# Attention and a two-layer MLP on one core: the last 64 rows of two batches leave in two output transfers, not in one

## The chip, the core and the metric

The kernel runs on one core of one Trainium2 chip. The metric is device time in microseconds (us) of one execution, as the median of several. The engines named below are TensorE (PE; its weight loads are PEld), VectorE (DVE), ScalarE (ACT), GpSimd (POOL) and SyncE (SP). SP computes nothing: it issues the DMA transfers, one after the other in program order. Sixteen DMA engines carry them out.

## The reference

Four batches, 12 heads, 448 rows, head size 64, all in float32. Softcapped attention is followed by a two-layer MLP with a leaky activation:

```python
scores = np.matmul(q, k.transpose(0, 1, 3, 2)) / np.sqrt(64)
scores = cap * np.tanh(scores / cap)
attn = softmax(scores)                      # row maximum taken off, 1e-9 added to the sum
x = np.matmul(attn, v)                      # (4, 12, 448, 64) -> rows of (1792, 768)
h = x @ w_in                                # 768 -> 2048
g = np.maximum(h, 0.0) + alpha * np.minimum(h, 0.0)
out = g @ w_out                             # 2048 -> 768, float32 (1792, 768)
```

## The kernel before, in words

Everything is computed in 16-bit halves: a float32 operand is split into a high and a low float16 part, and three products stand for one. The work of a batch has three stages: attention for 6 pairs of heads, `mm1` (x times w_in, 16 groups of 18 matmuls, line 965), and `mm2` (g times w_out, 48 matmuls for 128 rows and half of the 768 columns, line 1006). Attention of batch b runs beside `mm2` of batch b-1 and `mm1` of batch b, so that PE has work while DVE, ACT and POOL work on the softmax.

In the attention, rows of the softmax are split into the buffers `pw0`, `pw1` and `pw2` (lines 429 to 445), and SP turns them with a DMA transpose into `ptall` (line 720). A `pw` buffer is written again only after its transpose has landed. The product with v (PV, 24 matmuls of line 780) reads `ptall`. For the q and k of a coming pair, DVE takes a maximum over `rqk` (line 398), and PE turns it (line 415).

A batch has 448 rows: three blocks of 128 (t = 0, 1, 2) and 64 left over. The 64 rows left over of two batches (0 and 1, 2 and 3) are put together into a fourth block (t = 3) of 128 rows, which is computed once for both, after the second of them. So t = 3 occurs twice: for batches 0 and 1 in the middle of the program, and for batches 2 and 3 as its very last block. The results of a block are scaled into an SBUF buffer `osb` of 128 partitions (a part of the `wp` tile), and leave for HBM by SP.

Row s of a batch sits in `out` so that s = 112 c + p goes to row 4 p + c of the batch: each partition writes one run of 768 (or 384) floats, and neighbouring partitions write four rows apart. `out_rows(b, t0, m)` cuts m rows from t0 at the borders of c. For t < 3 that makes two transfers for each block (112 and 16, 96 and 32, 80 and 48 partitions). At t = 3 the kernel before makes one transfer of a destination with two blocks, batch b-1 and batch b, 64 rows each. In the middle of the program it carries all 768 columns (384 KB); at the end each half of 384 columns leaves by itself (192 KB each).

The order of all instructions comes from a planner (`Plan.order`): it plays the program through with estimated times, and each engine takes the ready operation of the smallest priority number. An SP operation has such estimates, too, so one more of them moves what the planner does afterwards. The order on each engine is fixed when the program is built; on the chip an engine waits at an instruction until what it needs is there.

Of the kernel before, what the change touches and what calls it, by code (L numbers as in the profile page):

```python
# [51 lines left out]
EVAC_P = -930.96  # L52
# [42 lines left out]
class Plan:  # L95
# [16 lines left out]
    def op(self, prio, times, fn, r=(), w=(), rows=1.0, port=True, mode=0, first=0.0):  # L112
        o = lambda: None
        o.first = first
        o.prio, o.times, o.fn, o.rows, o.idx, o.port, o.mode = prio + OFF[self.tag], times, fn, rows, len(self.ops), port, mode
        o.handles, deps = [], set()
        for write, regions in ((False, r), (True, w)):
            for x in regions:
                if isinstance(x, Handle):
                    if x not in o.handles:  # L120
                        o.handles.append(x)
                        x.ops.append(o)
                    x = (x, 0, 1)
                space, lo, hi = x
                old = self.acc.setdefault(space, [])
                deps.update(e[2] for e in old if e[0] < hi and lo < e[1] and (write or e[3]))
                if write:
                    old[:] = [e for e in old if e[0] < lo or hi < e[1]]
        for write, regions in ((False, r), (True, w)):
            for x in regions:  # L130
                space, lo, hi = (x, 0, 1) if isinstance(x, Handle) else x
                self.acc[space].append((lo, hi, o.idx, write))
        o.deps = len(deps)
        o.next = []
        for d in deps:
            self.ops[d].next.append(o)
        self.ops.append(o)
        return o
# [141 lines left out]
def kernel(  # L280
# [11 lines left out]
    nc = tc.nc  # L292
    B, H, S, D = q.shape
    DM, DFF = w_in.shape
    P = 128
    NCH = 4
    CP = S // NCH
    NPAIR = H // 2
    QP = P // 2
# [75 lines left out]
    op = plan.op  # L375
# [57 lines left out]
    def scaled(e, o, i, s):  # L433
        if e == "act":
            nc.scalar.activation(out=o, in_=i, func=AF.Copy, scale=s)  # L435
        elif e == "pool":
            nc.gpsimd.tensor_scalar(out=o, in0=i, scalar1=s, scalar2=1.0, op0=ALU.mult, op1=ALU.mult)
        else:
            nc.vector.tensor_scalar(out=o, in0=i, scalar1=s, scalar2=None, op0=ALU.mult)
# [7 lines left out]
    def either(n, psum=False, f=False, pool=False):  # L447

        t = {"act": (170 if psum else 200) + 93 * f + 0.833 * n, "dve": 155 + 50 * f + 1.05 * n if psum else 175 + 65 * f + 0.47 * n}
        if pool:  # L450
            t["pool"] = 260 + 0.842 * n if f else 190 + 0.817 * n
        return t
# [535 lines left out]
    def out_rows(b, t0, m):  # L988
        c = t0 // CP
        while m:  # L990
            p = t0 - c * CP
            k_ = min(m, CP - p)
            yield t0, k_, out[b * S:(b + 1) * S].rearrange("(p c) e -> c p e", c=NCH)[c, p:p + k_]
            t0, m, c = t0 + k_, m - k_, c + 1

    def room_r(j):
        return (("wp", j // 2), j % 2 * DM, j % 2 * DM + DM)

    def mm2(b, t, hf, prio):
        h = plan.handle("m")  # L1000

        def prods(e, part):
            for j in range(part * 4, part * 4 + 4):
                w = wo[j].rearrange("p (e c) -> p e c", e=2)
                for z, d in PRODS:
                    nc.tensor.matmul(ps_p[h.slot][:, :NH], g[j][:, d, t * P:(t + 1) * P], w[:, z, hf * NH:(hf + 1) * NH],  # L1006
                                     start=(j == 0 and z == d), stop=(j == NF - 1 and z == 1))

        oscs = [(("osc", b), 0, 1), (("osc", b - 1 if t == 3 else b), 0, 1)]
        for part in range(4):  # L1010
            js = range(part * 4, part * 4 + 4)
            op(prio, {"pe": 12 * 162.5}, lambda e, part=part: prods(e, part), w=[h],
               r=oscs + [room_r(wo_room[j]) for j in js] + [(("g", j), d * GW + t * P, d * GW + (t + 1) * P) for j in js for d in range(2)])
        os = NF - 2 + t % 2
        osb, (sp, lo, _) = room[os], room_r(os)
        a = cols = slice(hf * NH, (hf + 1) * NH)
        osr = (sp, lo + hf * NH, lo + (hf + 1) * NH)
        osc = vb[b].osc if t < 3 else joint[:, b // 2:b // 2 + 1]
        op(EVAC_P + prio * 1e-4, either(NH, True, f=True), lambda e: scaled(e, osb[:, cols], ps_p[h.slot][:, :NH], osc),
           r=[h, *oscs], w=[osr], port=False)  # L1020
        last = b == B - 1 and t == 3
        if hf == 0 and not last:
            return
        if not last:
            a, osr = slice(0, DM), room_r(os)
        if t == 3:
            p0, both_b = 3 * P - (NCH - 1) * CP, out[(b - 1) * S:(b + 1) * S].rearrange("(i p c) e -> c i p e", i=2, c=NCH)
            op(EVAC_P, {"sp": (550, 1000, 800)}, lambda e: nc.sync.dma_start(
                out=both_b[NCH - 1, :, p0:, a], in_=osb[:, a]), r=[osr])
            return  # L1030
        p = 0
        for t0, m, dst in out_rows(b, t * P, P):
            op(EVAC_P, {"sp": (550, 1000, 800)}, lambda e, p=p, m=m, dst=dst: nc.sync.dma_start(
                out=dst[:, a], in_=osb[p:p + m, a]), r=[osr])
            p += m


    def src_wi(j):
# [168 lines left out]
    def mm2_batch(b):  # L1207
        plan.tag = 151 + b
        x = 0
        for t in range(4):  # L1210
            for hf in range(2 if t < 3 or b % 2 else 0):
                mm2(b, t, hf, 1000 * (2 * b + 2) + x)
                x += 1
# [74 lines left out]
```

## Time and profile before

| | |
|---|---|
| median of 3 runs | 689.98 us (689.7 to 779.5) |
| the profiled execution | 690.83 us |
| its span, first to last instruction | 689.1 us |
| PE busy | 656.9 us, 95% of the span |
| DVE, ACT, POOL busy | 464.7, 419.2 and 264.2 us |
| DMA moved | 87.06 MB, mean 126 GB/s |

The span is what the profile can explain; 1.7 us of the profiled execution lie around it, and that execution is 0.85 us above the median. "Busy" says little about where an engine waits: for that the chain of waits and the stretches below are read. All times in rows are microseconds from the span's start.

### The profile page before, as it was taken

To read this page: it belongs to the slowest core of one execution; us is meant where nothing else is said; L and a number is where in the kernel's file an instruction comes from. 1 tells how busy PE (TensorE), PEld (TensorE's weight loads), DVE (VectorE), ACT (ScalarE), POOL (GpSimd) and SP (SyncE) were. 2 spreads that over 40 slices of the span, in tenths; PEclk is the share of its full clock that TensorE was granted. 3 is DMA by queue.
4 is the path that set the end of the run, shared out by engine and by line. 5 is a ranking of instruction groups with operands and counts; after the bars stand their busy time and mean duration, and the time that the engine had idled before them with its cause. 6 is when DMAs were issued, how large, how long until landed. Compare 5 with 4: busy or idle time off the path is not lost.

```text
span 689.1 us, 13358 instructions
## 1 busy us (share of the span) xinstructions
PE 656.9 (95%) x5042; PEld 412.0 (60%) x5042; DVE 464.7 (67%) x884; ACT 419.2 (61%) x867; POOL 264.2 (38%) x394
## 2 busy tenths in 40 slices
PE   8999999799999999999999999689999999999994
PEld 8877767678876555444555555335555655556662
DVE  2799999999899768988878698387873004440000
ACT  2868999989799857678657586467782013330000
POOL 0224555357776625678445364245550000000000
PEclk9999999999999999999999999889999999999998
DMA  8997663946554698976589998956766000000000
GB/s 223 268 280 231 178 211 90 245 133 153 131 91 100 128 175 184 173 143 113 95 173 186 181 201 119 120 119 119 127 109 114 23 19 7 1 1 24 23 24 23
DMA packets 189958, 87.06 MB, mean 126 GB/s; under 512 B 156166, under 2 KB 186182, under 8 KB 189894
## 3 DMA queue, kind: packets, MB, share of 16 engines
q1 hardware_dynamic: 189750, 86.22, 58.5%
q8 instruction: 39, 0.64, 0.4%
q14 instruction: 25, 0.20, 0.1%
q10 hardware_dynamic: 144, 0.00, 0.0%
HBM read 45.82 MB, written 5.51 MB: 74 GB/s over the span
## 4 chain that ended last, share of the span: by engine, by line
PE 68%; DVE 14%; DMA 10%; ACT 4%; issue 2%; SPq 1%; POOL 0%; ACTq 0%; DVEq 0%; POOLq 0%
PE p L1006 24%; PE p L965 24%; DMA ptall<-pw 8%; PE p L780 5%; PE s L588 3%; DVE mxs L623 3%; PE s L582 2%; PE p L807 2%; DVE wp L1069 2%; PE p L734 2%; DVE wp L1075 2%; PE p L1240 2%; PE p L546 2%; DVE wp L1065 1%; DMA wp<-in_moe_w_out_dram 1%
## 5 line engine op out<-in xcount | busy, mean ns | idle before, releaser
L965 PE MATMUL p<-xring,wi 128*128 128x448 f16 (+2 forms) x1440 | 227.2, 317 | 0.9 <-DVE vam L398 0.7
L1006 PE MATMUL p<-wp,gall 128*128 128x384 f16 x1344 | 223.4, 326 | 0.0
L965 PEld LDWEIGHTS <-wi 128*128 128x128 f16 x1440 | 135.8, 98 | 87.2 <-issue 8.7
L1006 PEld LDWEIGHTS <-gall 128*128 128x128 f16 x1344 | 129.8, 98 | 89.0 <-issue 4.9
L630 ACT ACTIVATE tall<-tall,mxs 128x448 f32<-128x448 f32 x126 | 82.8, 659 | 17.2 <-DVE mxs L625 8.6
L975 DVE SCALAR_TENSOR_TENSOR gr<-p,ca_g,gr 128x448 f32<-128x448 f32 (+2 forms) x80 | 46.8, 585 | 56.5 <-ACT gr L435 55.6
L623 DVE TENSOR_REDUCE mxs<-tall 128x2 f32<-128x896 f32 x63 | 67.7, 1078 | 6.4 <-ACT tall L619 6.1
L625 POOL TENSOR_SCALAR mxs<-mxs,small 128x2 f32<-128x2 f32 x62 | 32.4, 522 | 68.2 <-DVE mxs L623 54.8
L442 POOL TENSOR_TENSOR pw<-tall,pw 128x448 f16<-128x448 f32 x42 | 47.1, 1123 | 26.0 <-ACT pw L429 21.1
L435 ACT ACTIVATE wp<-p,small 128x384 f32<-128x384 f32 x21 | 12.1, 577 | 67.2 <-PE p L1006 67.2
L435 ACT ACTIVATE gr<-p,cs_g 128x448 f32<-128x448 f32 (+2 forms) x55 | 30.3, 550 | 33.9 <-PE p L965 33.6
L619 ACT ACTIVATE tall<-s,ams 128x896 f32<-128x896 f32 x42 | 41.5, 996 | 9.7 <-PE s L588 4.5
L649 POOL TENSOR_SCALAR rr<-sums 128x2 f32<-128x2 f32 (+2 forms) x70 | 23.5, 336 | 61.2 <-ACT tall L630 44.0
L429 ACT ACTIVATE pw<-tall 128x448 f16<-128x448 f32 x53 | 30.1, 572 | 24.0 <-DMA ptall<-pw 22.5
L780 PE MATMUL p<-ptall,vs 112*64 112x448 f16 x384 | 41.2, 355 | 1.9 <-DMA ptall<-pw 1.9
L429 ACT ACTIVATE gall<-gr 128x384 f16<-128x384 f32 (+4 forms) x61 | 28.0, 465 | 22.7 <-DVE gr L975 22.4
L442 DVE TENSOR_TENSOR pw<-tall,pw 128x448 f16<-128x448 f32 x42 | 29.1, 692 | 18.8 <-POOL pw L431 10.0
L442 POOL TENSOR_TENSOR gall<-gr,gall 128x256 f16<-128x256 f32 (+4 forms) x47 | 35.3, 754 | 9.4 <-ACT gall L429 7.7
L435 ACT ACTIVATE tall<-tall,rr 128x448 f32<-128x448 f32 x41 | 26.7, 663 | 19.0 <-DVE rr L652 19.0
L442 DVE TENSOR_TENSOR gall<-gr,gall 128x384 f16<-128x384 f32 (+4 forms) x65 | 31.6, 488 | 8.8 <-ACT gall L429 5.1
L780 PEld LDWEIGHTS <-vs 112*64 112x64 f16 x384 | 21.6, 109 | 19.8 <-issue 6.6
L588 PE MATMUL s<-qkTs 64*128 64x448 f16 (+1 forms) x288 | 28.1, 352 | 0.0
(175 smaller groups left out, 976.1 us busy)
## 6 DMA issues: line engine op xcount, KB each, us to landing
wp<-in_moe_w_in_dram SPq DMA_DIRECT2D x16, 768.0 KB, 6.4
wp<-in_moe_w_out_dram SPq DMA_DIRECT2D x16, 768.0 KB, 6.3
rvs<-in_v_dram SPq DMA_DIRECT2D x38, 224.0 KB, 3.3
rqk<-in_q_dram SPq DMA_DIRECT2D x12, 224.0 KB, 3.1
rqk<-in_k_dram SPq DMA_DIRECT2D x12, 224.0 KB, 3.6
ptall<-pw SPq DMA_TRANSPOSE x128, 3.2
wp<-in_q_dram SPq DMA_DIRECT2D x6, 224.0 KB, 5.9
wp<-in_k_dram SPq DMA_DIRECT2D x6, 224.0 KB, 8.5
```

Source lines behind the costliest of these rows:

```text
L429: nc.scalar.activation(out=o, in_=i, func=AF.Copy)
L435: nc.scalar.activation(out=o, in_=i, func=AF.Copy, scale=s)
L442: (nc.gpsimd if e == "pool" else nc.vector).tensor_tensor(out=o, in0=a, in1=b, op=ALU.subtract)
L588: yield lambda z=z, w=w: nc.tensor.matmul(s[rows, x, :S], q[a, z * S + cols.start:z * S + cols.stop], q[a, w * S:(w + 1) * S], start=(z == ...
L619: op(pr, {"act": (152 if reg else 245) + 377 * 2}, lambda e: nc.scalar.activation(out=t, in_=s[:, :, :S].rearrange("p c (j k) -> p c j k", ...
L623: op(pr, {"dve": 136 + 469 * 2}, lambda e: nc.vector.tensor_reduce(out=mt, in_=t, axis=AX.XY, op=ALU.max), r=tr, w=[mr], port=False)
L625: op(pr, {"dve": 200, "pool": 265}, lambda e: (nc.gpsimd if e == "pool" else nc.vector).tensor_scalar(out=mt, in0=mt, scalar1=ncap, scalar ...
L630: nc.scalar.activation(out=t[:, x], in_=t[:, x], func=AF.Exp, scale=capr, bias=mt[:, x:x + 1], accum_out=sums[:, u.idx % 3, col + x:col + ...
L780: nc.tensor.matmul(pv[x * D:(x + 1) * D, :n], vs[:, z, c:c + D], u.pt[x][:CP, y * NCH + kc], start=(i == 0), stop=(i == len(prods) - 1))
L965: nc.tensor.matmul(ps_p[h.slot][:, :n], w[:, z, kk, :], x[:, d, o:o + n], start=(kk == 0 and z == d), stop=(kk == NPAIR - 1 and z == 1))
L975: op(pr, {"dve": 198 + 1.07 * n}, lambda e: nc.vector.scalar_tensor_tensor(out=t, in0=ps_p[h.slot][:, :n], scalar=ca_g[:, j:j + 1], in1=t, ...
L1006: nc.tensor.matmul(ps_p[h.slot][:, :NH], g[j][:, d, t * P:(t + 1) * P], w[:, z, hf * NH:(hf + 1) * NH], start=(j == 0 and z == d), stop=(j ...
```

## The change

At t = 3 the special case goes. The 128 rows are now cut by the same loop as for other blocks, once for the 64 rows of batch b-1 and once for those of batch b, so that each batch has a transfer of its own: 64 partitions, 64 rows of `out`. The program has three transfers more: one more in the middle (two of 192 KB for one of 384 KB), and two more at the end (four of 96 KB for two of 192 KB). The bytes, their places and the run of each partition are the same.

```diff
-        if t == 3:
-            p0, both_b = 3 * P - (NCH - 1) * CP, out[(b - 1) * S:(b + 1) * S].rearrange("(i p c) e -> c i p e", i=2, c=NCH)
-            op(EVAC_P, {"sp": (550, 1000, 800)}, lambda e: nc.sync.dma_start(
-                out=both_b[NCH - 1, :, p0:, a], in_=osb[:, a]), r=[osr])
-            return
         p = 0
-        for t0, m, dst in out_rows(b, t * P, P):
-            op(EVAC_P, {"sp": (550, 1000, 800)}, lambda e, p=p, m=m, dst=dst: nc.sync.dma_start(
-                out=dst[:, a], in_=osb[p:p + m, a]), r=[osr])
-            p += m
+        for rows in [out_rows(b, t * P, P)] if t < 3 else [out_rows(b - 1, 3 * P, QP), out_rows(b, 3 * P, QP)]:
+            for t0, m, dst in rows:
+                op(EVAC_P, {"sp": (550, 1000, 800)}, lambda e, p=p, m=m, dst=dst: nc.sync.dma_start(
+                    out=dst[:, a], in_=osb[p:p + m, a]), r=[osr])
+                p += m
```

What the change does to the order on the engines was read from the two built programs. Before the middle transfer nothing differs. On SP the two smaller transfers stand where the one stood; behind them follow the same transpose of `pw2` and the same loads of q, k and v, and the next difference on SP comes some 30 us later.

On DVE, ACT and POOL the planner's choices differ from the first operations behind that place on. DVE before, from the last operation of 436 us on (`p_63`, `p_64` and `p_66` are banks with results of `mm1`, `gr` and `gall` take them up, `pw_104`, `pw_105` and `pw_106` are the three softmax buffers; L398 is the maximum over `rqk` for which PE's L415 waits):

```order
L439 TENSOR_SCALAR tall<-tall,rr 128x448
L442 TENSOR_TENSOR pw_106<-tall,pw_106 128x4x112
L652 RECIPROCAL rr<-rr 128x2
L439 TENSOR_SCALAR gr<-p_63,cs_g 128x448
L442 TENSOR_TENSOR pw_104<-tall,pw_104 128x4x112
L975 SCALAR_TENSOR_TENSOR gr<-p_63,ca_g,gr 128x448
L398 TENSOR_REDUCE small<-rqk 112x2
L411 TENSOR_REDUCE mxt<-p_65 2x1
L413 TENSOR_SCALAR mxt<-ident,mxt 2x2
L975 SCALAR_TENSOR_TENSOR gr<-p_64,ca_g,gr 128x448
L442 TENSOR_TENSOR gall<-gr,gall 128x448
L445 SCALAR_TENSOR_TENSOR pw_106<-tall,rr,pw_106 128x4x112
```

And now:

```order
L439 TENSOR_SCALAR tall<-tall,rr 128x448
L652 RECIPROCAL rr<-rr 128x2
L442 TENSOR_TENSOR gall<-gr,gall 128x448
L439 TENSOR_SCALAR gr<-p_63,cs_g 128x448
L975 SCALAR_TENSOR_TENSOR gr<-p_63,ca_g,gr 128x448
L398 TENSOR_REDUCE small<-rqk 112x2
L442 TENSOR_TENSOR gall<-gr,gall 128x448
L439 TENSOR_SCALAR gr<-p_64,cs_g 128x448
L411 TENSOR_REDUCE mxt<-p_65 2x1
L413 TENSOR_SCALAR mxt<-ident,mxt 2x2
L975 SCALAR_TENSOR_TENSOR gr<-p_64,ca_g,gr 128x448
L442 TENSOR_TENSOR gall<-gr,gall 128x448
```

The two differences L442 into `pw` have left DVE (POOL has them now), so that none of them stands ahead of L398; two L442 into `gall` and one L439 have come in their place.

On PE the order is the same until the last groups of batch 3's attention, from about 496 us of the trace of before on: there three PV groups and the `mm1` group of `wi15` change places with their neighbours. The last of that on SP is where the attention of batch 3 ends and the outputs of batch 2 begin. SP before:

```order
L720 DMA_TRANSPOSE ptall<-pw_106 128x8x128
L720 DMA_TRANSPOSE ptall<-pw_104 128x8x128
L720 DMA_TRANSPOSE ptall<-pw_106 128x8x128
L1033 DMA out_dram<-wp_100 112x768
L1033 DMA out_dram<-wp_100 16x768
L720 DMA_TRANSPOSE ptall<-pw_104 128x8x128
L1033 DMA out_dram<-wp_100 96x768
```

And now:

```order
L720 DMA_TRANSPOSE ptall<-pw_105 128x8x128
L1029 DMA out_dram<-wp_100 112x768
L1029 DMA out_dram<-wp_100 16x768
L720 DMA_TRANSPOSE ptall<-pw_106 128x8x128
L720 DMA_TRANSPOSE ptall<-pw_104 128x8x128
L720 DMA_TRANSPOSE ptall<-pw_106 128x8x128
L720 DMA_TRANSPOSE ptall<-pw_104 128x8x128
L1029 DMA out_dram<-wp_100 96x768
```

Four transposes instead of one now stand behind the first two outputs of batch 2. On PE the last PV group, which needs the last of them, has moved to 168 `mm2` matmuls and one other PV group after the start of batch 2's `mm2`.

## Rows read from the trace of the kernel before

**Rows 1.** The page's first line.

```profile
span 689.1 us, 13358 instructions
```

**Rows 2.** Waits of PE, whole span: engine, line, waited for: us, times, longest.

```profile
PE p L415 <- DVE small L398: 9.5, 2, 9.0
...
PE p L780 <- DMA ptall<-pw: 1.9, 5, 0.8
```

**Rows 3.** Stretches: length, then what the first line lists.

```profile
core 0: us, PE busy (x) PEld busy (x) DVE busy (x) ACT busy (x) POOL busy (x), PEclk, DMA share, GB/s
...
440.00:450.00 10.00, 1.20 (x7) 0.39 (x5) 3.63 (x6) 2.37 (x4) 2.99 (x5) 0.72 0.90 184
450.00:465.00 15.00, 14.76 (x98) 6.69 (x98) 11.86 (x24) 9.15 (x18) 7.24 (x11) 0.85 0.50 97
...
679.00:689.10 10.10, 0.00 (x0) 0.00 (x0) 0.00 (x0) 0.58 (x1) 0.00 (x0) 0.71 0.11 38
```

**Rows 4.** PE in order of time: start, us, operation, [idle before it, released by].

```profile
430.82 10.38 PE L965 MATMUL p<-xring,wi 128*128 128x448 f16 x54
450.24 0.34 PE L415 MATMUL p<-ident,small 112*2 112x112 f32 x1 [9.04 <-DVE small L398]
```

**Rows 5.** SP in order of time at the middle transfer: start, us.

```profile
432.11 0.67 SPq L1028 DMA_DIRECT2D out_dram<-wp  x1
432.87 7.09 SPq L720 DMA_TRANSPOSE ptall<-pw  x1
```

**Rows 6.** Chain of waits, 415 to 480 us: start, us, what.

```profile
432.87 12.77 DMA ptall<-pw
...
448.96 1.14 DVE small L398
...
450.58 5.42 PE p L965 x18
...
457.35 2.39 PE p L780 x24
...
460.43 3.51 PE p L965 x18
```

**Rows 7.** Stretches of 2 us, columns as in Rows 3.

```profile
440.00:442.00 2.00, 1.20 (x7) 0.39 (x5) 0.00 (x0) 0.00 (x0) 0.00 (x0) 1.00 0.13 52
...
684.00:686.00 2.00, 0.00 (x0) 0.00 (x0) 0.00 (x0) 0.00 (x0) 0.00 (x0) 0.50 0.13 51
...
664.00:666.00 2.00, 2.00 (x14) 1.22 (x13) 0.00 (x0) 0.01 (x1) 0.00 (x0) 1.00 0.56 151
```

**Rows 8.** SP in order of time at two outputs of another block.

```profile
407.30 0.81 SPq L1033 DMA_DIRECT2D out_dram<-wp  x2
408.20 1.31 SPq L720 DMA_TRANSPOSE ptall<-pw  x1
```

**Rows 9.** Chain of waits, 465 to 600 us.

```profile
509.06 7.80 PE p L1006 x48
...
526.80 0.47 DVE pw L439
527.29 0.69 DVE pw L445
...
530.42 3.69 DMA ptall<-pw
```

**Rows 10.** Line 720, SP's transposes: issue to landing over the whole span.

```profile
DMA to landing us min/median/max: 2.6/3.2/6.7
```

**Rows 11.** The end of the program in order of time: ACT, then SP.

```profile
679.02 0.58 ACT L435 ACTIVATE wp<-p,joint 128x384 f32<-128x384 f32 x1 [1.38 <-PE p L1006]
677.67 2.47 SPq L1028 DMA_DIRECT2D out_dram<-wp  x2
```

**Rows 12.** Line 1033, outputs of other blocks: issue to landing.

```profile
DMA to landing us min/median/max: 2.5/2.8/3.6
```

**Rows 13.** Line 1283, the program's end: ns min/median/max, first and last start.

```profile
L1283 SPq DRAIN x3: 7/7/7, 688.3 to 688.6; - x3
```

## The prediction

> **What bounds the kernel now.** The page's first line gives a span of 689.1 us [rows 1]; the execution took 690.83 us. I asked first for PE's waits, since PE is busy for 95% of the span. Over the whole span two of them matter here [rows 2]: one of 9.0 us at L415, for a maximum that DVE takes (L398), and some small ones of PV (L780) for transposes, the longest 0.8 us.
>
> The table by stretches places the first [rows 3]: in 440 to 450 us PE is busy for 1.2 us, and so is nothing else for more than 3.7 us. The granted clock falls to 0.72 there and is 0.85 in the 15 us behind it. The table's last line is the other place: the final 10.1 us hold 0.58 us of ACT and nothing else but DMA.
>
> What holds up DVE at 441 us? SP's order of time shows it [rows 5]: L1028, the output with two blocks, is issued at 432.11, and the transpose behind it occupies SP for 7.09 us, where the one behind two outputs of another block took 1.31 [rows 8]. The chain of waits goes through the same transpose: 12.77 us from issue to landing, to 445.64, then POOL and DVE, L398 to 450.10, and PE's L415 [rows 6, 4].
>
> Why that transpose? The stretches of 2 us say [rows 7]. In 440 to 442 us the DMA share is 0.13 at 52 GB/s. Two engines of sixteen, fully busy, are 2/16 = 0.125. In 664 to 666 us, while outputs of the other kind leave, it is 0.56 at 151 GB/s. So the destination of two blocks leaves through two DMA engines at some 25 GB/s each: 384 KB take 384 / 50 = 7.7 us, and whatever has a share on those two engines queues behind. At the end the same: 0.13 and 51 GB/s in 684 to 686 us, 5 us after the last computation.
>
> **The change, term by term.** *The middle.* Two outputs are issued in 0.81 us [rows 8] instead of one in 0.67, so the transpose goes about 0.15 us later, at 433.0. In the chain a transpose right behind two outputs landed 3.69 us after its issue [rows 9]; that makes 436.7 instead of 445.64. The loads of q and k behind it on SP no longer wait for a 7 us issue either. In the new order DVE also has no `pw` operation ahead of L398, and both ways L398 is done before PE's third `mm1` group ends, at 430.82 + 10.38 = 441.20 [rows 4]. L415 then follows at once instead of at 450.24: 9.0 us.
>
> How much of it is there at the next PV? Before, it started 457.35 - 450.24 = 7.1 us after L415 [rows 6, 4]. In these, PE at the lower clock lost 5.42 - 3.51 = 1.9 us on a group of 18 matmuls [rows 6] and 0.24 on L415 (0.34 against some 0.1). Without the pause the clock should stay up; but this PV waits for a transpose that comes out of DVE's operations between L411 and L445, and these don't run on PE's clock. So I leave the 7.1 us as they are: PE waits there up to 2.1 us for `ptall` in place of running slowly. **9.0 us** are taken; the upper end is 9.0 + 2.1 = 11.1 us. The lower end takes the slowest landing of a transpose, 6.7 us [rows 10], 3.0 us more, of which DVE's new order hides part: 7 us.
>
> From that PV to about 496 us PE's order is unchanged. PE had no pause there before, so all is earlier by the same amount.
>
> *The end.* The last ACT operation ends at 679.60, and SP's last issue, part of the row from 677.67 on, ends 0.5 us behind it [rows 11]. Now two issues follow, the second about 0.45 us after the first, at 680.05. Outputs of other blocks land 2.5 to 3.6 us after issue, median 2.8 [rows 12]: 682.85. SP's drains start at 688.3 and the span ends at 689.1, so 0.8 us of closing follow [rows 13], with 0.1 before: 683.75, **5.3 us** earlier; 4.5 to 5.6 by the ends of that row. The first pair, two matmul groups earlier, is out of the way by then.
>
> No row shows a transfer of 64 partitions. The nearest are those of 80 and 48 in rows 12, among others, which is why I take their landing. The Trainium skill, "DMA: Bandwidth & Descriptors", section "Why a DMA increments its semaphore by 16 and not by 1", says that a transfer gets the largest number of engines up to 16 that divides the slowest dimension of both sides; by it a first dimension of 2 gives 2 engines, and 64 gives 16. The share of 0.13 agrees with the first; the second no run here shows yet.
>
> *The new order.* From 496 us on the last PV of batch 3 stands later on PE: `mm2` starts at 509.06, 168 matmuls at 7.80 / 48 = 0.1625 us are 27.3, one PV is 2.4 [rows 9, 6]: 538.8, all in the old time. The transposes it needs: the first of the four behind the outputs goes where the one went before, at 530.4, the second 1.3 later. The buffers are written again after 3.2 us for landing [rows 10] and 0.47 + 0.69 us on DVE [rows 9]; so the last goes at 531.7 + 4.4 = 536.1 and lands 3.7 later, at 539.8. That is a wait of 1.0 us in place of 0.8 [rows 2]. `mm2` now also takes the bank of `wi15` about 3 us after PE has left it, with two passes over it in between. I take **0.5 us lost** for the new order: none of the old waits and none of the new at one end (0.8 gained), each of three PV groups 1.3 us late at the other (4 lost). SP's third and further issues cost nothing of their own: nothing else is queued on SP at the end, and in the middle the 0.15 us are counted.
>
> **Sum.** 690.83 - 9.0 - 5.3 + 0.5 = 677.0 us for the profiled execution. That stood 0.85 us above the median of 689.98, so the runs should show **676.2 us**. A measurement of this kernel can tell about 2% from no change; 2% less than 689.98 is 676.2, so the forecast lies on the border.
>
> **Rivals.** *The clock's loss comes back too*: the PV's transposes are early enough, the middle gives 11.1 us, and the new order gains its 0.8 us: 689.98 - 11.1 - 5.3 - 0.8 = 672.8. For it: DVE is done with L398 earlier than before. Against: PE's waits for `ptall` show that PV usually comes just after its transposes.
>
> *Only the end gains*: the middle's 9 us come up again further on, since DVE was busy for 11.86 of the 15 us behind the pause [rows 3], and a new order may make PE wait for it. 689.98 - 5.3 = 684.7. Against: DVE, ACT and POOL all stood still with PE in the pause, so none had work to catch up with.
>
> *The split gives nothing.* Two transfers run one after the other on the same engines, and the second issue is only added: 0.15 us in the middle and 0.45 at the end, 690.6. Rows 7 speak against it: two of sixteen engines are at work, and a second transfer can only use more. The Trainium skill, same page, section "Rules for kernel authors", advises against this change: two transfers to disjoint partition halves serialize, use one of 128 partitions. Its reason is that both halves already go over all 16 engines; a share of 0.13 in this trace says that this is not so here, so little of the chance goes to it.
>
> *Slower*: SP stands at the first output of batch 2 until its results are scaled, with four transposes behind it. Each us that this is late beyond some 1 us goes into the last PV, and PE waits with nothing else ahead in its order. The gains of 14.3 us are used up when the outputs are about 13 us late: 12 us of pause, and 2.1 us of clock, as after the pause of 9 us in the trace [rows 3, 6]. Late by 27 us it would be 2% slower, 704 us. Against: before, the transpose behind these outputs went at 530.4, 3.3 us after PE was done with the results (509.06 + 96 x 0.1625 + 2.4 = 527.1) [rows 9, 6].
>
> **Chances and range.** The forecast 0.67, by its bounds from 673 to 680; the clock too 0.12; only the end 0.14; nothing 0.04; slower 0.03, some of it beyond 2%. The range goes from 672.0 to 684.9 and so takes in the first three. Of the forecast about half lies under 676.2; with the clock's case that makes faster by over 2% 0.46, within 2% 0.52, slower 0.02.
>
> **What would show it.** In the profile of the changed kernel: SP's transpose behind the two outputs at 432 us takes 1.3 us instead of 7.09; PE's wait at L415 is gone or under 1 us, and a wait of up to 2 us for `ptall` stands at the next PV; no stretch has a DMA share of 0.13 for some us; the granted clock is 1.00 in 440 to 465; and the span ends 4 to 5 us after the last ACT operation, not 9.5. The prediction is wrong if the outputs of 64 partitions still run on two engines, if L415 waits for something else as long, or if PE has new pauses of some us between 460 and 560 us.

## The result, and the profile after

The changed kernel takes 672.1 us, median of four runs (670.31 to 673.27). Of the four runs of the kernel before one was slow, at 779.5 us, and is left out; the other three have a median of 689.98 us. The ratio of the means is 0.9734, 95% interval 0.9702 to 0.9766. So it is faster by more than 2%, for which the chance given was 0.46. The forecast was 676.2 us, with a range from 672.0 to 684.9: the result is 4.1 us faster than the forecast and lies inside the range by 0.1 us.

The profiled execution took 671.53 us. First the page's first line, then the stretches that answer to [rows 3], with their columns:

```profile
span 669.7 us, 13360 instructions
```

```profile
430.00:440.00 10.00, 10.00 (x54) 5.09 (x53) 8.02 (x15) 7.31 (x16) 5.34 (x10) 1.00 1.07 215
440.00:450.00 10.00, 10.00 (x79) 4.88 (x78) 8.37 (x18) 6.35 (x12) 4.48 (x7) 1.00 0.73 133
450.00:465.00 15.00, 15.00 (x87) 7.52 (x85) 14.34 (x24) 11.78 (x25) 11.71 (x16) 1.00 0.76 149
```

Where PE was busy for 1.2 us of 10, it is now busy for all 10, and the granted clock is 1.00 throughout. From 400 us to the end, PE's list of waits is empty. SP in order of time at the middle transfers, the answer to [rows 5]:

```profile
430.23 1.18 SPq L1029 DMA_DIRECT2D out_dram<-wp  x2
431.51 1.33 SPq L720 DMA_TRANSPOSE ptall<-pw  x1
432.94 0.68 SPq L462 DMA_DIRECT2D rqk<-in_q_dram  x1
```

The transpose behind the two outputs takes SP 1.33 us in place of 7.09. PE in order of time, for [rows 4], and DVE beside it:

```profile
429.03 10.38 PE L965 MATMUL p<-xring,wi 128*128 128x448 f16 x54
439.36 0.26 PE L415 MATMUL p<-ident,small 112*2 112x112 f32 x1
...
444.30 2.46 PE L780 MATMUL p<-ptall,vs 112*64 112x448 f16 x24
```

```profile
437.99 1.22 DVE L398 TENSOR_REDUCE small<-rqk 112x2 f32<-112x1024 f32 x1 [0.55 <-DMA rqk<-in_k_dram]
...
444.11 0.69 DVE L445 SCALAR_TENSOR_TENSOR pw<-tall,rr,pw 128x448 f16<-128x448 f32 x1 [0.95 <-ACT pw L435]
```

L415 follows the third `mm1` group at once, and PV some 5 us after it, where 7.1 us lay between them before. The chain of waits, which [rows 6] show of before, has that PV at:

```profile
444.37 2.39 PE p L780 x24
```

The end of the program, for [rows 11] and [rows 7]: ACT and SP in order of time, and one stretch of 2 us.

```profile
663.97 3.07 SPq L1029 DMA_DIRECT2D out_dram<-wp  x4
665.32 0.58 ACT L435 ACTIVATE wp<-p,joint 128x384 f32<-128x384 f32 x1 [1.38 <-PE p L1006]
```

```profile
666.00:668.00 2.00, 0.00 (x0) 0.00 (x0) 0.00 (x0) 0.00 (x0) 0.00 (x0) 1.00 0.51 109
```

The last outputs leave at a DMA share of 0.51 and 109 GB/s, not 0.13 and 51, and the span ends 669.7 - 665.9 = 3.8 us after the last ACT operation instead of 9.5.

The two spans differ by 19.35 us. Laid out along PE, from the three `mm1` groups before L415 on (PV by the chain of waits):

| part | before | after | gained, us |
|---|---|---|---|
| start of the three `mm1` groups | 430.82 | 429.03 | 1.79 |
| from there to L415 | 19.42 | 10.33 | 9.09 |
| L415 to PV | 7.11 | 5.01 | 2.10 |
| PV to the end of the last ACT operation | 222.25 | 221.53 | 0.72 |
| from there to the end of the span | 9.45 | 3.80 | 5.65 |

The first row is no effect of the change: up to there both programs are the same. In the ten profiles of this study the middle output is issued between 430.23 and 432.13 us, whatever the kernel, so single profiles differ by up to 1.9 us there. Without that row the table gives 17.56 us; the medians of the runs differ by 17.9.

### The profile page after: what moved, and what is told of

Read it like the earlier page. It is cut to its first block, busy times and chain, and to the rows that moved or that the text cites. A ratio compares the mean times of both kernels' runs of the same rounds, so it can differ in the third digit from the quotient of the medians.

```text
span 669.7 us, 13360 instructions
## 1 busy us (share of the span) xinstructions
PE 652.8 (97%) x5042; PEld 409.5 (61%) x5042; DVE 466.5 (70%) x887; ACT 419.8 (63%) x865; POOL 264.1 (39%) x393
## 4 chain that ended last, share of the span: by engine, by line
PE 78%; DVE 9%; ACT 6%; DMA 5%; issue 2%; POOL 0%; ACTq 0%; SPq 0%; DVEq 0%; POOLq 0%
PE p L1006 29%; PE p L965 26%; PE p L780 5%; DMA ptall<-pw 4%; PE s L588 4%; PE s L582 3%; PE p L807 3%; PE p L1236 2%; PE p L734 2%; DVE mxs L623 2%; PE p L546 2%; ACT tall L630 1%; DVE wp L1065 1%; DVE wp L1071 1%; DMA rvs<-in_v_dram 1%
## 5 line engine op out<-in xcount | busy, mean ns | idle before, releaser
L625 POOL TENSOR_SCALAR mxs<-mxs,small 128x2 f32<-128x2 f32 x59 | 30.5, 517 | 68.7 <-DVE mxs L623 56.1
L442 POOL TENSOR_TENSOR pw<-tall,pw 128x448 f16<-128x448 f32 x41 | 46.4, 1133 | 18.8 <-ACT pw L429 13.2
L435 ACT ACTIVATE wp<-p,small 128x384 f32<-128x384 f32 x22 | 12.7, 577 | 63.5 <-PE p L1006 63.5
L435 ACT ACTIVATE gr<-p,cs_g 128x448 f32<-128x448 f32 (+2 forms) x55 | 30.3, 550 | 30.5 <-PE p L965 30.1
L442 DVE TENSOR_TENSOR pw<-tall,pw 128x448 f16<-128x448 f32 x43 | 29.8, 692 | 14.0 <-ACT pw L429 12.0
L442 DVE TENSOR_TENSOR gall<-gr,gall 128x64 f16<-128x64 f32 (+4 forms) x66 | 32.9, 499 | 6.2 <-ACT gall L429 3.2
L442 POOL TENSOR_TENSOR gall<-gr,gall 128x256 f16<-128x256 f32 (+4 forms) x46 | 34.0, 742 | 5.6 <-ACT gall L429 3.5
L435 ACT ACTIVATE tall<-tall,rr 128x448 f32<-128x448 f32 x42 | 27.0, 660 | 8.3 <-DVE rr L652 7.3
```

Of the source, the lines that this page charges most:

```text
L442: (nc.gpsimd if e == "pool" else nc.vector).tensor_tensor(out=o, in0=a, in1=b, op=ALU.subtract)
L625: op(pr, {"dve": 200, "pool": 265}, lambda e: (nc.gpsimd if e == "pool" else nc.vector).tensor_scalar(out=mt, in0=mt, scalar1=ncap, scalar ...
```

## Experiments

The theory: the outermost dimension of the destination sets how many DMA engines carry a transfer; 2 blocks mean two engines, and what stands behind on SP waits for them. The rivals: it takes two transfers; or the planner's new order makes the gain; or the end is just the closing of the program. All ratios are of the means of runs, against runs of the kernel before on the same chip.

**The two places apart.** Only the middle split (the last block keeps the old transfer):

```diff
-        if t == 3:
+        if t == 3 and last:
```

(with the changed kernel's loop behind it). Expected: "

> Only the middle transfer is split; the last block leaves as before, so the order on all engines is that of the changed kernel. Theory (a destination whose outermost dimension is 2 uses two DMA engines, and each place costs by itself): the middle's 9.1 us pause and the clock's 2.1 us go, the 9.5 us from the last ACT operation to the span's end stay; about 5.6 us above the changed kernel, 677 to 678 us. Rival (the end's gain hangs on the middle, or the middle's comes back later): under 674 or over 683 us.

"

Measured: 677.24 us, ratio 0.9825 (0.9799 to 0.985). PE waits for nothing from 400 us on, and the end is the old one, 675.2 - 665.8 = 9.4 us behind ACT:

```profile
663.86 2.49 SPq L1028 DMA_DIRECT2D out_dram<-wp  x2
665.22 0.58 ACT L435 ACTIVATE wp<-p,joint 128x384 f32<-128x384 f32 x1 [1.38 <-PE p L1006]
```

Only the end split (`if t == 3 and not last:`). Expected: "

> Only the last block's transfers are split; the middle one stays, and the order on all engines is that of the kernel before. Theory: SP's transpose behind the middle output still takes about 7 us and L415 still waits 9 us; the span ends 3.8 us after the last ACT operation in place of 9.5; 5.6 us gained, about 684.5 us. Rival (closing the program takes the time, not the transfers): no gain, 690 us.

"

Measured: 684.38 us, ratio 0.9919 (0.9894 to 0.9944). The middle is as before, first by PE's waits, then by SP's order of time:

```profile
PE p L415 <- DVE small L398: 9.1, 1, 9.1
```

```profile
431.61 0.68 SPq L1028 DMA_DIRECT2D out_dram<-wp  x1
432.39 7.16 SPq L720 DMA_TRANSPOSE ptall<-pw  x1
```

The last ACT operation ends at 679.15:

```profile
678.57 0.58 ACT L435 ACTIVATE wp<-p,joint 128x384 f32<-128x384 f32 x1 [1.38 <-PE p L1006]
```

The span ends 682.9 - 679.15 = 3.75 us behind it. The two gains add up: 1.75% and 0.81% are 2.56%, against 2.66% for both. Each place costs by itself, and the end is not the closing of the program.

**The order apart from the transfers.** The planner sees one operation, which issues both new transfers; all engines keep the order of the kernel before:

```diff
+            def both(e):
+                p = 0
+                for bb in (b - 1, b):
+                    for t0, m, dst in out_rows(bb, 3 * P, QP):
+                        nc.sync.dma_start(out=dst[:, a], in_=osb[p:p + m, a])
+                        p += m
+            op(EVAC_P, {"sp": (550, 1000, 800)}, both, r=[osr])
```

Expected: "

> Both places are split, but the planner sees one operation with both transfers in it, so that every engine keeps the order of the kernel before. Theory (the engines of the transfer): SP's transpose behind the outputs takes 1.3 us and L415's wait is under 1 us; PV after it may wait up to 2.1 us for its transpose, since in this order DVE has two pw differences ahead of L398; 673 to 677 us. Rival (the new order made the gain in the middle): L415 still waits some 9 us and only the end gains, 684.5 us.

"

Measured: 673.17 us, ratio 0.9756 (0.9733 to 0.978). SP's transpose behind the outputs takes 1.33 us. PE's waits from 400 us on are two; then PE and DVE around the PV behind L415, in order of time:

```profile
PE p L780 <- DMA ptall<-pw: 1.3, 1, 1.3
PE p L415 <- DVE small L398: 0.5, 1, 0.5
```

```profile
440.19 0.26 PE L415 MATMUL p<-ident,small 112*2 112x112 f32 x1 [0.47 <-DVE small L398]
...
445.13 2.46 PE L780 MATMUL p<-ptall,vs 112*64 112x448 f16 x24
```

```profile
444.55 0.69 DVE L445 SCALAR_TENSOR_TENSOR pw<-tall,rr,pw 128x448 f16<-128x448 f32 x1 [0.90 <-ACT pw L435]
```

The old order has the gain of the middle but for the 0.5 us at L415, since L398 ends 0.3 us behind PE's third `mm1` group. The wait of 1.3 us is that of another PV, at 522 us: the one of 0.8 us in [rows 2], which the new order does not have. The PV behind L415 did not wait, against the expectation: it starts while DVE is still at L445, so it does not need that result. Between this ratio and that of the changed kernel the intervals overlap, so the times do not settle what the new order is worth. The profiles do better. From the start of that PV (by PE's order of time) to the end of the last ACT operation, the four profiles in the old order (before, end only, this one, and the single transfer below) take 222.3 to 222.8 us, and the six in the new order 221.2 to 221.6. In that stretch the old order has PE's wait of 0.8 to 1.3 us for the last PV's transpose, and the new order has none.

Then the reverse, the new order with the old transfer: two operations, of which the first issues the transfer of two blocks and the second nothing.

```diff
             op(EVAC_P, {"sp": (550, 1000, 800)}, lambda e: nc.sync.dma_start(
                 out=both_b[NCH - 1, :, p0:, a], in_=osb[:, a]), r=[osr])
+            op(EVAC_P, {"sp": (550, 1000, 800)}, lambda e: None, r=[osr])
             return
```

Expected: "

> The planner sees two operations at the last 64 rows, but the first issues the old transfer of two blocks and the second issues nothing: the new order with the old transfers. Theory (the engines of the transfer): SP's transpose behind it still takes about 7 us, the loads of q and k behind it land at about 446 us, L415 waits 6 to 9 us, the clock falls, and the end takes 9.5 us: 686 to 691 us. Rival (the new order made the gain in the middle): no wait at L415, 677 to 679 us.

"

Measured: 687.67 us, ratio 0.9968 (0.9949 to 0.9987). SP, DVE, and PE's waits:

```profile
431.81 7.17 SPq L720 DMA_TRANSPOSE ptall<-pw  x1
439.08 0.53 SPq L462 DMA_DIRECT2D rqk<-in_q_dram  x1
439.71 0.39 SPq L462 DMA_DIRECT2D rqk<-in_k_dram  x1
```

```profile
445.93 1.22 DVE L398 TENSOR_REDUCE small<-rqk 112x2 f32<-112x1024 f32 x1 [7.72 <-DMA rqk<-in_k_dram]
```

```profile
PE p L415 <- ACT rvs L435: 7.1, 1, 7.1
```

```profile
446.55 0.72 ACT L435 ACTIVATE rvs<-rvs,vam 112x512 f32<-112x512 f32 x1 [7.73 <-DMA rvs<-in_v_dram]
```

In this order no `pw` operation stands ahead of L398, and DVE waits there for the loads of k, which stood on SP behind the transpose that took 7.17 us. The list of waits names ACT's L435 instead, because that ended 0.1 us after L398 (447.27 and 447.15); it had waited as long, for the load of v behind the same transpose. So the pause has two ways through the same blocked queue: the `pw` buffer, and the loads. In this profile the new order shortens it by 2 us; it does not remove it.

**One transfer or two, and how many blocks.** One transfer again, with the 64 rows outermost and the batches inside:

```diff
-            p0, both_b = 3 * P - (NCH - 1) * CP, out[(b - 1) * S:(b + 1) * S].rearrange("(i p c) e -> c i p e", i=2, c=NCH)
+            p0, both_b = 3 * P - (NCH - 1) * CP, out[(b - 1) * S:(b + 1) * S].rearrange("(i p c) e -> p i c e", i=2, c=NCH)
-                out=both_b[NCH - 1, :, p0:, a], in_=osb[:, a]), r=[osr])
+                out=both_b[p0:, :, NCH - 1, a], in_=osb[:, a]), r=[osr])
```

Expected: "

> One transfer again for both batches, as before, but with the 64 rows as the outermost dimension of the destination and the two batches inside; the order on all engines is that of the kernel before. (It changes which row goes where: the partitions fill the destination in another order, so the last 64 rows of each batch are exchanged among themselves.) Theory (the size of the outermost dimension): the transpose behind it takes SP 1.3 us, no wait of 9 us, the span ends 3.3 to 3.8 us after the last ACT operation, 672 to 674 us. Rival (it takes two transfers): 690 us as before.

"

Measured: 672.13 us, ratio 0.9737 (0.9706 to 0.9769). SP in order of time, and one stretch of 2 us:

```profile
430.77 0.66 SPq L1028 DMA_DIRECT2D out_dram<-wp  x1
431.52 1.33 SPq L720 DMA_TRANSPOSE ptall<-pw  x1
```

```profile
432.00:434.00 2.00, 2.00 (x12) 1.06 (x11) 1.71 (x3) 1.78 (x6) 1.09 (x3) 1.00 1.01 276
```

The same number of transfers, bytes and rows as before, in the old order, and the whole gain. So it is not the splitting. (This kernel is no replacement as it stands, since it writes the last 64 rows of a batch to other places.)

The last three keep the changed kernel's two transfers and its order, and give each destination n blocks, n = 2, 4, 8 (here n = 4):

```diff
-                    out=dst[:, a], in_=osb[p:p + m, a]), r=[osr])
+                    out=dst[:, a] if t < 3 else dst[:, a].rearrange("(x n) e -> n x e", n=4), in_=osb[p:p + m, a]), r=[osr])
```

Expected for 2: "

> The changed kernel's transfers, one for each batch, but each with a destination of 2 blocks of 32 rows (every second row in a block; rows are exchanged within a batch). The order is the new one. Theory: 384 KB on two engines again, 7.7 us, a DMA share of 0.13, a pause of about 7 us at L415 as with the old transfer in the new order, and 9.5 us at the end: 686 to 690 us. Rival (two transfers suffice): 672 us.

"

Expected for 4: "

> As the last, with 4 blocks of 16 rows for each transfer (rows exchanged within a batch). Theory: four engines, a DMA share of 0.25, about 100 GB/s, 384 KB in 3.8 us; L415 waits some 7.1 - 3.8 = 3.3 us, the clock falls for a part of it, the end is about 1 us longer than in the changed kernel: 675 to 678 us. Rival (any larger number of blocks gives all engines): 672 us.

"

Expected for 8: "

> As the last, with 8 blocks of 8 rows for each transfer (rows exchanged within a batch). Theory: eight engines, a DMA share of 0.5, about 200 GB/s, 384 KB in 1.9 us; L415 waits 0 to 1.5 us, the end is some 0.4 us longer than in the changed kernel: 672 to 674 us. Rival: as with 4 blocks, 676 us.

"

Measured for 2: 689.65 us, ratio 0.9996 (0.9983 to 1.001). SP; the end (columns as in Rows 3); PE's waits:

```profile
433.48 7.41 SPq L720 DMA_TRANSPOSE ptall<-pw  x1
```

```profile
682.00:684.00 2.00, 0.00 (x0) 0.00 (x0) 0.00 (x0) 0.00 (x0) 0.00 (x0) 0.58 0.13 49
```

```profile
PE p L415 <- DVE small L398: 9.4, 1, 9.4
```

For 4: 680.26 us, ratio 0.9862 (0.9835 to 0.989). The same three:

```profile
432.43 4.37 SPq L720 DMA_TRANSPOSE ptall<-pw  x1
```

```profile
673.00:675.00 2.00, 0.00 (x0) 0.00 (x0) 0.00 (x0) 0.00 (x0) 0.00 (x0) 1.00 0.27 89
```

```profile
PE p L415 <- DVE small L398: 4.2, 1, 4.2
```

For 8: 673.88 us, ratio 0.9762 (0.9738 to 0.9787). SP and PE's waits:

```profile
432.95 2.66 SPq L720 DMA_TRANSPOSE ptall<-pw  x1
```

```profile
PE p L415 <- DVE small L398: 1.4, 1, 1.4
```

The busiest microsecond at its end:

```profile
668.00:669.00 1.00, 0.00 (x0) 0.00 (x0) 0.00 (x0) 0.16 (x1) 0.00 (x0) 1.00 0.45 141
```

| outermost dimension of the destination | SP at the next transpose, us | wait at L415, us | span's end behind ACT, us | time, us |
|---|---|---|---|---|
| 2 (two transfers) | 7.41 | 9.4 | 10.0 | 689.65 |
| 4 (two transfers) | 4.37 | 4.2 | 5.8 | 680.26 |
| 8 (two transfers) | 2.66 | 1.4 | 4.3 | 673.88 |
| 64 (two transfers, the change) | 1.33 | 0 | 3.8 | 672.1 |
| 64 (one transfer, old order) | 1.33 | 0 | 3.2 | 672.13 |

All four columns follow the outermost dimension, and beside it the number of transfers matters little: with 2 blocks the split gains nothing. There the share at the end stays at 0.13 although two transfers are issued for each half, so the second does not bring engines of its own. The expectation for 4 was too low by 2 to 5 us: it took 384 KB at 100 GB/s, the end shows 89, the pause was 4.2 and not 3.3 us, and the end 2.0 us longer than in the changed kernel and not 1. For 8 the time came as expected, but the 200 GB/s did not show: the busiest microsecond has 141.

For 2 blocks the pause is 2.3 us longer with two transfers in the new order (9.4) than with one (7.1). PE's three `mm1` groups, the load of k and the chain through L398, first with one transfer (PE), then with two (PE, chain):

```profile
429.79 10.38 PE L965 MATMUL p<-xring,wi 128*128 128x448 f16 x54
```

```profile
430.73 10.38 PE L965 MATMUL p<-xring,wi 128*128 128x448 f16 x54
```

```profile
441.62 7.45 DMA rqk<-in_k_dram
...
449.09 1.23 DVE small L398
```

Counted from the start of the groups, the load of k is issued 9.9 us later with one transfer (439.71) and 10.9 with two (441.62), and it takes some 6.2 us to land (445.93, when L398 starts) against 7.45. So 1.0 us comes from the later issue and 1.2 from the slower landing. Why it lands more slowly stays open.

No run beat the changed kernel beyond its interval; the single transfer with 64 rows outermost equals it in time.

## Why the prediction was right, point by point

**Two engines.** Right as far as shares and rates can show it, since no view here names the engines: the share of 0.13 in [rows 7] becomes 0.27 with 4 blocks at the end, and 51 GB/s become 89. The Trainium skill's rule on the number of engines ("DMA: Bandwidth & Descriptors", "Why a DMA increments its semaphore by 16 and not by 1") gives 2, 4 and 8 for these blocks; the shares of 0.13 and 0.27 agree for two and four, and of 8 and 64 the runs show only that SP's stand at the next transpose shrinks further, to 2.66 and 1.33 us. The advice in the same page's "Rules for kernel authors" against two transfers to partition halves does not decide here: one transfer and two take the same time once the outermost dimension is 64.

**The middle, 9.0 us at L415.** Measured 9.09 us. The steps held: SP's transpose took 1.33 us, and PE was bound by its own third group, but narrowly. L398 ended at 439.21, 0.2 us before that group; in the old order it ended 0.3 us behind it and PE waited 0.5 us, where the text had it done in time "both ways". The two outputs took SP 1.18 us and not 0.81; that cost nothing, since PE was still in its groups.

**L415 to PV, the mis-sized term.** The text left the 7.1 us as they were, "this PV waits for a transpose that comes out of DVE's operations between L411 and L445". It does not: in the changed kernel, and with the old order, it starts while DVE is at L445. The wait of up to 2 us for `ptall`, named as a sign, did not appear. The clock's loss came back whole, 2.10 us, the upper end that the text gave with 2.1. With the old order and the new transfers the gap was 445.13 - 440.19 = 4.9 us, so that the 2.1 us more of the old trace were PE's slow group and no late transpose.

**The end, 5.3 us.** Measured 5.65, just above the row's bound of 5.6. The text took a landing of 2.8 us from other outputs. In the run with the new transfers in the old order, one line (L1031) issues the six transfers of 64 partitions and nothing else, and their median is lower:

```profile
DMA to landing us min/median/max: 2.1/2.2/3.0
```

**The new order, 0.5 us lost.** Measured 0.72 us gained from PV on: the last PV, now later in PE's order, has no wait in the list, where 1.0 us was expected. With the old order and the new transfers that wait was 1.3 us. The 4 us at the text's other end, three PV groups late by 1.3 us each, did not occur: none of them has a wait.

**The sum.** 14.3 - 0.5 = 13.8 us were forecast. 2.1 more from the clock, 1.2 from the order, 0.35 at the end and 0.09 in the middle make 17.5 us, and with the 1.79 us by which the two profiles differ ahead of the change that is the 19.3 of the spans. The case that came true is the rival "the clock's loss comes back too", 672.8 us, to which the text gave 0.12. Its argument against, that PV usually comes just after its transposes, was taken from other PVs. So the mechanism was right in both places, but the sum was not: 672.1 us lies below the bounds of the forecast's own case (673 to 680), and two of the four runs lie below the whole range. That the median falls inside it is partly luck.

**The other rivals.** Only the end gains: false, the middle's gain is still there at the end of the span. The split gives nothing: true with 2 blocks, false with 64 rows. The argument against it, that a second transfer can only use more engines, was wrong: with 2 blocks the share stays at 0.13. What helped was the longer outermost dimension that the split brought with it. Slower: the last PV has no wait behind SP's four transposes.

## What to carry to other kernels

A DMA share that stands at 2/16 for some microseconds, with bytes still flowing, was the sign of a transfer on two engines here: look at its outermost dimension before its size. Order the dimensions so that a long one is outermost (64 here; 8 came close in time, 4 and 2 did not), and count what stands behind such a transfer on the issuing queue: in the middle that cost 9.1 us of pause and 2.1 of clock, against 5.65 us at the end, where nothing stood behind. When a pause goes, add back what the lower clock took from the work behind it, unless a row of that very wait shows another limit.

## What the runs showed that was not expected

A transfer of few blocks held up the issue of the transpose behind it, not only its landing: SP stood at that transpose for 1.33, 2.66, 4.37 and 7.41 us with 64, 8, 4 and 2 blocks, and the loads behind it were issued only afterwards. What in the issue waits is not shown. And a program that is the same up to there reached the middle output at 430.23 us in one profile and at 432.13 in another, a scatter of 1.9 us that is larger than the 0.7 to 1.6 us that the new order gains behind that PV.
